# A second level of Strassen in product 4 of both tiles, one more residual by accumulating DMA, and weight loads planned around the accumulations

## The chip, the cores and the metric

The kernel runs on one core of a Trainium2 chip. The metric is the device time of one launch in microseconds (us): the median of several runs. A profile is taken of one execution; its span goes from the first to the last instruction on the core.

The core has a matrix engine (TensorE, PE in the profile; PEld is its loading of weights), a vector engine (VectorE, DVE), a scalar engine (ScalarE, ACT), GpSimd (POOL) and a synchronising engine (SyncE, SP) that here only issues DMAs. Each runs its own list of instructions in order and waits on semaphores for the others. Matrix results go to PSUM, in banks of 128 x 512 floats.

## The reference

A deep cross network of six layers over 16384 rows of 1024 values, with `x0` the input:

```python
x = x0                                   # [16384, 1024] bf16
for l in range(6):
    proj = einsum('bd,de->be', x, ws[l]) + bs[l]     # ws[l]: [1024, 1024]
    x = x0 * proj + x
```

So each layer is one product with a 1024 x 1024 matrix, a bias, a product with `x0` and a residual.

## The kernel before

**Tiling.** The rows are split into 16 pairs of 512-row tiles, 1024 rows a pair. All data is kept transposed (features on partitions). A pair's `x` is a 2 x 2 of blocks: feature half by row tile. Two pairs make a group, and the group's two pairs are called lanes 0 and 1 (the change's words call them tiles). The kernel runs 96 *units*, one layer of one pair, in the order group, layer, lane: layer 0 of lane 0, layer 0 of lane 1, layer 1 of lane 0 and so on. A group is 12 units. The three buffers of `x` (`xst`) and of `x0` (`x0T`) rotate over the pairs.

**One unit.** The 2 x 2 block product is done with seven products instead of eight (the Winograd form of Strassen's algorithm). Their names are P1 to P7. DVE makes the differences T1 to T4 of input blocks; TensorE multiplies them with weights or with sums of weights, which group 0 makes once and saves to device memory (`Lc`). P1, P6, P7 accumulate on each other in four PSUM banks `pA`; each is 16 matmuls of 512 columns (four for each of the output blocks m: P1.0 to P1.3). Products 5, 2 and 3 go one *level* deeper: each is again seven products of half size, 28 matmuls of 256 columns in all, on the banks `pX` (5 and 3 on pX0 and pX1, 2 on pX2 and pX3). The pieces are named 5p1 to 5p7 and so on. Their inputs are made by DVE (5t13, 5t2, 5t4; 23t2 and 23t4 for products 2 and 3 together). ACT evicts PSUM: `biased` (line 335, instruction at 337) adds the bias and writes E1, E6, E7, E4; `copy` (line 326) writes the pieces' results (e_p5, e_c11, e_u0, e_u1, e_c21) and copies bank to bank (f1, f2). DVE then adds the correction `cc`. Product 4 is a 512-column product (P4.0 to P4.3, evicted by E4) or, where `K4` (line 152) lists the lane for a layer, a two-level one (4p1 to 4p7, with 4t13, 4t2, 4t4, 4cc and the add Wa in place of the accumulation on `pA`), on pX2 and pX3. Before, `K4` lists both lanes in layer 0, lane 1 alone in layers 1 to 4, and none in layer 5; group 0 keeps one level.

**End of a unit.** DVE adds products into four result blocks Q, U, V, W (Q1, Ua, Ub, Va, Wa; lines 547 to 555), multiplies each by `x0` (Qm, Um, Vm, Wm) and adds the residual: by DVE (Qx and so on, line 566) or, for the blocks in `DMA_RES` (line 153), by an accumulating DMA that POOL issues (line 563). W is block 21 (second feature half, first row tile). Before, Q, U and V go by DMA in layers 1 to 4, and W by DVE. In layer 0 the products go straight to the buffer, and in layer 5 DVE adds all four. The result is the input of the same lane's next layer, two units later.

**Buffers.** Seven evict buffers hold 5c, 3c (products 5 and 3), U, V, W, Q and P1s (product 1). From unit to unit the names change places by `NEXT` (line 176).

**Order.** Everything is first recorded as an `Op` with an engine, a duration, what it reads and writes. The order on TensorE is written out by hand: `PE_TWO` for units with one-level product 4, `PE_FOUR` for two-level ones, others for the first units and the last. `schedule` (line 51) lays all operations out by these durations, taking on each engine the ready one that is due first; the program is emitted in that order, so every engine has a fixed order. Weights go through a ring of 12 slots of 512 KB (`RING`): 11 loads for each layer of a group (10 in layer 5), in the order of `ring_seq` (line 225). `pump` (line 239) is called after every emitted operation and issues the next load on SP as soon as its slot's last use has been emitted. SP also has the transposing loads of `x0` (`ld`), the output's transposes (`tro`) and stores (`sto`).

Of the kernel before, what the change touches and what calls it, by code (L numbers as in the profile page):

```python
# [20 lines left out]
PE_ONE = """  # L21
# [1 line left out]
P3.0 P4.3 P4.1 P4.0 P4.2  # L23
""".split()
PE_TWO = """
5p5 P1.1 5p1 P1.0 P1.3 5p2 2p5 5p6 2p1 P1.2 5p3 2p2 5p7 2p6 P6.0 5p4 2p3 3p5 2p7 3p1 P6.1 2p4 3p2 3p6 P6.2 P6.3 3p3
3p7 P7.0 P7.1 P7.2 3p4 P7.3 P4.1 P4.0 P4.3 P4.2
""".split()
PE_FOUR = """
5p5 P1.0 5p1 2p5 2p1 P1.1 5p2 5p6 2p2 P1.2 2p6 P1.3 5p3 5p7 2p3 2p7 P6.0 3p5 5p4 2p4 P6.1 P6.3 3p1 4p5 P6.2 4p1 3p2  # L30
P7.0 4p2 3p6 4p6 P7.1 3p3 4p3 4p7 P7.2 3p7 4p4 P7.3 3p4
""".split()
PE_LAST = """
P1.0 P1.1 P1.2 P1.3 P2.0 P2.1 P2.2 P2.3 P5.0 P5.1 P5.2 P5.3 P6.0 P6.1 P6.2 P6.3 P3.0 P3.1 P3.2 P3.3 P7.0 P7.1 P7.2 P7.3
# [2 lines left out]
ARRIVE = {"rows0": 4.9, "w0.1": 6.4, "rows1": 8.9, "rows2": 11.3, "w0.2": 11.9, "h0": 14.3, "h1": 15.5, "q": 17.5, "next": 21.0, "raw1": 40.0}  # L37


ACCUM = 9.0  # L40


class Op:
# [81 lines left out]
    return order, start, late  # L125


@with_exitstack
def kernel(
    ctx: ExitStack,  # L130
# [18 lines left out]
    KQ, HQ, NQ = KH // 2, H // 2, NB // 2  # L149
    RING = 12  # L150
    NDUMMY = 8
    K4 = {0: (0, 1), 1: (1,), 2: (1,), 3: (1,), 4: (1,)}
    DMA_RES = {1: "QUV", 2: "QUV", 3: "QUV", 4: "QUV"}

    const = ctx.enter_context(tc.tile_pool(name="const", bufs=1))
    dram = ctx.enter_context(tc.tile_pool(name="dram", bufs=1, space=bass.MemoryType.DRAM))
# [16 lines left out]
    ip["4"] = ip["2"]  # L173
    P1s, P5s, Q, U, V, W, C3 = (work.tile([P, KH, KH, P], BF16, name=f"ev{i}") for i in range(7))
    EV = {"5c": P5s, "3c": C3, "U": U, "V": V, "W": W, "Q": Q, "P1s": P1s}
    NEXT = {"5c": "3c", "3c": "5c", "U": "W", "V": "U", "W": "V", "Q": "Q", "P1s": "P1s"}
    home = {r: r for r in EV}
    TURNED, rows = ((0, 0), (1, 0), (0, 1)), (P1s, U, V)
    zeros = tin["4"][:, 0]
# [41 lines left out]
    for gl in range(NGROUP * L):  # L221
        if gl < L:
            ring_seq += [(gl, w, "load") for w in RAW] + [(gl, w, "make") for w in MADE]
        else:
            ring_seq += [(gl, w, "load") for w in "1 5 5i 2 2i 6 3 3i 7 4 4i".split()[:11 if gl % L in K4 else 10]]
    slot = {(gl, w): f"slot{i % RING}" for i, (gl, w, _) in enumerate(ring_seq)}
    wt, uses_left, live = {}, {}, []
    pos = {"next": 0}
# [7 lines left out]
        live.append(key)  # L236
        return wt[key]

    def pump():
        while pos["next"] < len(ring_seq):  # L240
            gl, w, kind = ring_seq[pos["next"]]
            if kind == "make":
                return
            t = ring_tile((gl, w))
            if t is None:
                return
            nc.sync.dma_start(t[:], w_src(gl % L, w))
            pos["next"] += 1

    def ring_make(gl, w):  # L250
# [27 lines left out]
    for u, (pr, l) in enumerate(units):  # L278
# [12 lines left out]
        kmajor = l == 0  # L291
        inn = "" if one else "5234" if lane in K4.get(l, ()) and grp > 0 else "523"
        ISW = [ISN[w] for w in ISLOT] + [f"is.{w}.{i}" for w in ISLOT for i in "5637"] if pr == 2 else []
        line = {w: i for i, w in enumerate(PE_FIRST if first else PE_LAST if last else PE_ONE if one else PE_FOUR if lane in K4.get(l, ()) and pr > 1 else PE_TWO)}

        def pe(name, occ, fn, rd, wr, weights=(), u=u, gl=gl, line=line, at=0.0):
            op(f"{name}@{u}", "PE", occ, occ + 0.19, fn, rd, wr, [(gl, w) for w in weights], key=(u, line[name]), at=at)
# [15 lines left out]
        def group(name, w, bank, bname, rhs, rname, m, start, gl=gl, kmajor=kmajor):  # L313
            def fn():
                for k in range(KH):
                    r = rhs[:, k, :] if kmajor else rhs[:, :, k, :]
                    o = bank[:] if kmajor else bank[:].rearrange("p (j r) -> p j r", r=P)
                    nc.tensor.matmul(o, lhsT=wt[(gl, w)][:, k, m * P:(m + 1) * P], rhs=r,  # L318
                                     start=(start and k == 0), stop=(k == KH - 1), skip_group_check=True)
            if first and name in ("P5.0", "P5.1"):  # L320
                rname = rname + ["w0.5a"]
            else:
                rname = rname + wname(w)
            pe(name, 0.863, fn, rname, [bname], [w], at={"1": ARRIVE["w0.1"], "2": ARRIVE["w0.2"]}.get(w, 0.0) if first else 0.0)
# [151 lines left out]
        if not one:  # L476
            for X, a, b in (("5", 0, 1), ("2", 2, 3), ("3", 0, 1), ("4", 2, 3))[:len(inn)]:
                Bm, src = SRC[X]
                C, pn = CB[X], Pn[X]
                if kmajor:  # L480
                    q = lambda dh, n, k, Bm=Bm: Bm[:, dh * KQ + k, n * NQ:(n + 1) * NQ]
                    tk = lambda i, k, X=X: tin[X].rearrange("p i (k b) -> p i k b", k=KQ)[:, i, k]
                else:
                    q = lambda dh, n, k, Bm=Bm: Bm[:, n * KQ:(n + 1) * KQ, dh * KQ + k, :]
                    tk = lambda i, k, X=X: tin[X].rearrange("p i (j k r) -> p i j k r", j=KQ, k=KQ)[:, i, :, k, :]
                c = lambda dh, n, C=C: C[:, n * KQ:(n + 1) * KQ, dh * KQ:(dh + 1) * KQ, :].rearrange("p j m r -> p m j r")
                cn = lambda dh, n, pn=pn: [pn(2 * dh) + f".{n}", pn(2 * dh + 1) + f".{n}"]
                call = [pn(m) for m in range(KH)]

                def inner(i, bank, start, X=X, gl=gl, q=q, tk=tk, src=src, kmajor=kmajor):  # L490
                    quad = {1: (0, 0), 2: (1, 0), 3: (1, 1)}
                    rhs = (lambda k: q(*quad[i], k)) if i in quad else (lambda k: tk({4: 3, 5: 0, 6: 2, 7: 1}[i], k))
                    rn = {1: src, 2: src, 3: src, 4: X + "t4", 5: X + "t13", 6: X + "t2", 7: X + "t13"}[i]
                    w = X if i in (1, 2, 4) else X + "i"

                    def fn():
                        if i in (1, 2, 4):
                            k0, e0 = {1: (0, 0), 2: (KQ, 0), 4: (KQ, HQ)}[i]
                            wv = wt[(gl, w)][:, k0:k0 + KQ, e0:e0 + HQ]
                        else:  # L500
                            wi = weight(gl, w) if gl < L else weight(gl, w)[:]
                            wv = wi.rearrange("p q (k e) -> p q k e", k=KQ)[:, {5: 0, 6: 1, 3: 2, 7: 3}[i]]
                        for m in range(KQ):
                            for k in range(KQ):
                                o = pX[bank][:, m * NQ:(m + 1) * NQ]
                                nc.tensor.matmul(o if kmajor else o.rearrange("p (j r) -> p j r", r=P), lhsT=wv[:, k, m * P:(m + 1) * P],  # L506
                                                 rhs=rhs(k), start=(start and m == 0 and k == 0), stop=(k == KQ - 1), skip_group_check=True)
# [39 lines left out]
        if not last:  # L547
            if not one:
                ttop("Q1", Q[:], Q[:], P1s[:], ADD, allm("Q") + allm("P1s"), allm("Q"))
            ttop("Ua", U[:], U[:], P5s[:], ADD, allm("U") + allm("5c"), allm("U"))  # L550
            if not one:
                ttop("Ub", U[:], U[:], C3[:], ADD, allm("U") + allm("3c"), allm("U"))
            if "4" in inn:
                ttop("Wa", W[:], W[:], V[:], ADD, allm("W") + allm("V"), allm("W"))
            ttop("Va", V[:], V[:], P5s[:], ADD, allm("V") + allm("5c"), allm("V"))
            for nm, C, q in (("Q", Q, (0, 0)), ("U", U, (0, 1)), ("V", V, (1, 1)), ("W", W, (1, 0))):
                if l == 0:
# [148 lines left out]
        load_half("4", h)  # L706
    nc.sync.dma_start_transpose(out=blk(x0Ts[0], 1, 1), in_=x0[NB:2 * NB, H:2 * H])

    held = [i for i in order if ops[i].name.startswith("ld") and ops[i].name.endswith(".1@1")]
    for i in held:  # L710
        ops[i].fn()
    for i in order:
        if i not in held:
            ops[i].fn()
        for k in ops[i].weights:
            if k in uses_left:
                uses_left[k] -= 1
        pump()


# [28 lines left out]
```

## Time and profile before

| | |
|---|---|
| median of 3 runs | 2222.31 us (2222.19 to 2222.82) |
| span of the profiled execution | 2220.2 us |
| PE busy | 2209.2 us, 14565 matmuls |
| PEld busy | 1421.3 us |
| DVE busy | 2133.0 us, 2502 instructions |
| ACT busy | 2035.8 us, 3627 instructions |
| POOL busy | 204.6 us |
| DMA | 478.66 MB, mean 216 GB/s |

The profile gives no launch time of its own for the profiled execution, only its span; 2220.2 us is 2.1 us below the median of the runs. In its lists of instructions an entry reads: line of the kernel, engine, operation, output <- inputs by the names of the tiles, shape, count. The list of waits reads: who waited, for whom, the total in us, how often, the longest. In the list by stretches each engine has its busy time and, in brackets, its instructions. A DMA's landing time counts from the start of the instruction that issues it.

### The profile page before, as it was taken

Reading aid. Unit: us, or ns where it says so; the run is one execution under the profiler, and the core shown is the slowest. Engines: PE = TensorE matmul, PEld = TensorE weight load, DVE = VectorE, ACT = ScalarE, POOL = GpSimd, SP = SyncE. Lnnn points to the kernel's source line nnn. Section 1 sums busy time; section 2 is a strip of 40 time slices with the busy share of each in tenths; the row PEclk is TensorE's granted clock in tenths of the full one; section 3 lists DMA queues with packets and bytes.
Section 4 is the critical chain, followed back from the end, with each engine's and each line's share of the span. In section 5 each row is a group of like instructions: output and inputs, shape, how many; then the busy total and the mean of one; then the engine's idle time right before and its main releaser. Section 6 shows DMA issues by size and latency. Waiting matters only on the chain.

```text
span 2220.2 us, 39424 instructions
## 1 busy us (share of the span) xinstructions
PE 2209.2 (100%) x14565; PEld 1421.3 (64%) x14565; DVE 2133.0 (96%) x2502; ACT 2035.8 (92%) x3627; POOL 204.6 (9%) x263
## 2 busy tenths in 40 slices
PE   9999999999999999999999999999999999999998
PEld 5555566666666666666666666666666666666664
DVE  8999999999999999999999999999999999999997
ACT  7888899999999999999999999999999999999997
POOL 1221100110001100011000110011100111001110
PEclk9999999999999999999999999999999999999999
DMA  9676879767996689966898679986789777897777
GB/s 275 206 204 188 214 202 257 198 174 206 257 258 181 171 226 252 255 176 176 234 250 243 171 189 239 252 223 177 207 232 251 217 179 224 221 259 190 202 224 163
DMA packets 454306, 478.66 MB, mean 216 GB/s; under 512 B 269024, under 2 KB 381152, under 8 KB 454112
## 3 DMA queue, kind: packets, MB, share of 16 engines
q1 hardware_dynamic: 418352, 349.49, 53.3%
q0 software_dynamic: 35168, 126.38, 28.0%
q8 instruction: 114, 1.87, 0.3%
q14 instruction: 80, 0.66, 0.1%
q10 hardware_dynamic: 592, 0.27, 0.0%
HBM read 252.72 MB, written 58.20 MB: 140 GB/s over the span
## 4 chain that ended last, share of the span: by engine, by line
PE 98%; DMA 1%; SPq 0%; DVE 0%; issue 0%; POOLq 0%; ACT 0%; DVEq 0%; ACTq 0%
PE pA L318 53%; PE pX L506 43%; PE pX L318 3%; DMA x0T<-in_x_dram 0%; DMA xst<-x0T 0%; SPq L690 0%; DVE ev L204 0%; SPq L697 0%; DVE x0T L204 0%; DVE T L204 0%; SPq L703 0%; POOLq L744 0%; ACT ev L337 0%; SPq L700 0%; DVEq L204 0%
## 5 line engine op out<-in xcount | busy, mean ns | idle before, releaser
L337 ACT ACTIVATE ev<-pA,b_all 128x512 bf16<-128x512 f32 x1311 | 898.6, 692 | 117.5 <-PE pA L318 78.2
L506 PEld LDWEIGHTS <-wp 128*128 128x128 bf16 x8364 | 818.4, 98 | 270.6 <-issue 1.0
L318 PE MATMUL pA<-T,wp 128*128 128x512 bf16 x3936 | 939.6, 379 | 0.0
L318 PEld LDWEIGHTS <-wp 128*128 128x128 bf16 x5808 | 568.0, 98 | 507.9 <-issue 2.2
L327 ACT CAST ev<-pX 128x512 bf16<-128x512 f32 x1264 | 690.1, 597 | 22.0 <-PE pX L506 14.9
L506 PE MATMUL pX<-ti,wp 128*128 128x256 bf16 x4728 | 655.8, 273 | 0.0
L204 DVE TENSOR_TENSOR ev<-ev,ev 128x2048 bf16<-128x2048 bf16 (+1 forms) x414 | 497.5, 1218 | 44.1 <-ACT ev L327 36.9
L204 DVE TENSOR_TENSOR ev<-ev,x0T 128x2048 bf16<-128x2048 bf16 (+1 forms) x324 | 386.4, 1210 | 1.7 <-ACT ev L337 0.3
L327 ACT COPY pX<-pX 128x512 f32<-128x512 f32 x618 | 359.7, 595 | 3.3
L318 PE MATMUL pA<-xst,wp 128*128 128x512 bf16 x1280 | 318.9, 379 | 0.0
L563 POOL DMA_DIRECT2D xst<-ev x192 | 165.8, 865 | 1292.0 <-ACT ev L337 506.9
L506 PE MATMUL pX<-xst,wp 128*128 128x256 bf16 x1736 | 260.4, 273 | 0.0
L506 PE MATMUL pX<-T,wp 128*128 128x256 bf16 x1548 | 232.2, 273 | 0.0
L204 DVE TENSOR_TENSOR ev<-ev,ip 128x1024 bf16<-128x1024 bf16 x309 | 207.7, 690 | 0.2 <-ACT ev L327 0.2
L204 DVE TENSOR_TENSOR T<-xst,T 128x2048 bf16<-128x2048 bf16 x160 | 195.7, 1223 | 2.4 <-PE pX L506 1.4
L204 DVE TENSOR_TENSOR T<-xst 128x2048 bf16<-128x2048 bf16 x160 | 195.6, 1223 | 1.7 <-PE pA L318 1.4
L327 ACT CAST ip<-pX 128x512 bf16<-128x512 f32 x309 | 182.3, 590 | 0.4 <-PE pX L506 0.4
L204 DVE TENSOR_TENSOR xst<-ev,xst 128x2048 bf16<-128x2048 bf16 x124 | 151.8, 1225 | 0.2
L204 DVE TENSOR_TENSOR ti<-T,ti 128x512 bf16<-128x512 bf16 x262 | 111.2, 424 | 0.2
L204 DVE TENSOR_TENSOR ti<-xst 128x1024 bf16<-128x1024 bf16 x148 | 102.3, 691 | 8.4 <-PE pX L506 8.0
L204 DVE TENSOR_TENSOR ti<-xst,ti 128x1024 bf16<-128x1024 bf16 x148 | 101.9, 689 | 0.1
L204 DVE TENSOR_TENSOR ti<-T 128x1024 bf16<-128x1024 bf16 x131 | 90.4, 690 | 0.1
(57 smaller groups left out, 679.2 us busy)
## 6 DMA issues: line engine op xcount, KB each, us to landing
wp<-Lc SPq DMA_DIRECT2D x329, 512.0 KB, 6.1
xst<-ev POOLq DMA_DIRECT2D x192, 512.0 KB, 5.2
wp<-in_ws_dram SPq DMA_DIRECT2D x148, 512.0 KB, 6.6
out_dram<-x0T SPq DMA_DIRECT2D x60, 512.0 KB, 4.3
Lc<-wp POOLq DMA_DIRECT2D x24, 512.0 KB, 5.1
Lc<-xst POOLq DMA_DIRECT2D x23, 512.0 KB, 5.4
ev<-in_x_dram SPq DMA_DIRECT2D x3, 512.0 KB, 6.1
wp<-in_ws_dram SPq DMA_DIRECT2D x4, 256.0 KB, 7.4
```

The source lines that it names most:

```text
L204: nc.vector.tensor_tensor(out=o, in0=a, in1=b, op=op)
L318: nc.tensor.matmul(o, lhsT=wt[(gl, w)][:, k, m * P:(m + 1) * P], rhs=r, start=(start and k == 0), stop=(k == KH - 1), skip_group_check=True)
L327: act(name, lambda: nc.scalar.copy(out=dst, in_=src), rd, wr)
L337: act(name, lambda: nc.scalar.activation(out=dst, in_=src, func=IDENT, bias=b_all[:, c:c + 1], scale=1.0), rd, wr, True)
L506: nc.tensor.matmul(o if kmajor else o.rearrange("p (j r) -> p j r", r=P), lhsT=wv[:, k, m * P:(m + 1) * P], rhs=rhs(k), start=(start and m ...
L563: nc.gpsimd.dma_start(xblk(xst, *q), C[:], accum_op=ADD)
```

## The change

1. `K4` lists both lanes in layers 0 to 4, so lane 0's product 4 has two levels in layers 1 to 4 too (groups 1 to 7).
2. `DMA_RES` holds W as well: block 21's residual is added by DMA in layers 1 to 4.
3. `plan_loads` gives each weight load from group 1 on a time before which it is not issued: after planned accumulations, but no later than `LEAD` and 1.5 `LOAD` ahead of its first planned use or of the next load's latest time. `pump` gets the time of the operation just emitted and holds loads back by it; a held load also waits for the newest matmul emitted.
4. The ring's order (`LOAD_ORDER`), `PE_TWO`, `PE_FOUR`, the planner's duration for an accumulation (`ACCUM`, 9.0 to 8.5), the rotation `NEXT` and the place of Ua among the recorded operations change. In the new rotation V keeps its buffer, U takes 5c's, 5c takes 3c's, 3c takes W's and W takes U's.

```diff
 PE_TWO = """
-5p5 P1.1 5p1 P1.0 P1.3 5p2 2p5 5p6 2p1 P1.2 5p3 2p2 5p7 2p6 P6.0 5p4 2p3 3p5 2p7 3p1 P6.1 2p4 3p2 3p6 P6.2 P6.3 3p3
-3p7 P7.0 P7.1 P7.2 3p4 P7.3 P4.1 P4.0 P4.3 P4.2
+2p5 5p5 P1.1 5p1 P1.0 P1.3 5p2 5p6 2p1 P1.2 5p3 2p2 5p7 2p6 P6.0 5p4 2p3 3p5 2p7 3p1 P6.1 2p4 P6.3 3p2 3p6 P6.2 P7.1
+3p7 3p3 P7.3 P7.0 3p4 P7.2 P4.0 P4.3 P4.2 P4.1
 PE_FOUR = """
-5p5 P1.0 5p1 2p5 2p1 P1.1 5p2 5p6 2p2 P1.2 2p6 P1.3 5p3 5p7 2p3 2p7 P6.0 3p5 5p4 2p4 P6.1 P6.3 3p1 4p5 P6.2 4p1 3p2
-P7.0 4p2 3p6 4p6 P7.1 3p3 4p3 4p7 P7.2 3p7 4p4 P7.3 3p4
+5p1 P1.0 5p5 P1.2 2p5 2p1 5p6 5p2 P1.1 2p6 2p2 P6.0 5p3 P1.3 5p7 2p3 3p5 2p7 P6.2 5p4 2p4 P6.1 P6.3 3p1 4p5 4p1 P7.0
+3p2 4p2 3p6 4p6 P7.1 3p3 4p3 3p7 4p7 P7.3 3p4 4p4 P7.2
-ACCUM = 9.0
+ACCUM = 8.5
+LOAD, BURST, LEAD = 1.45, 2.9, 5.0
+LOAD_ORDER = "1 5i 2i 5 2 6 3i 4i 3 4 7".split()
+def plan_loads(loads, bursts):
+    latest, nxt = [0.0] * len(loads), 1e9
+    for n in range(len(loads) - 1, -1, -1):
+        nxt = min(loads[n][1] - LEAD, nxt) - 1.5 * LOAD
+        latest[n] = nxt
+    busy, t = [], 0.0
+    for b in sorted(bursts):
+        t = max(t, b + 1.0)
+        busy.append((t, t + BURST))
+        t += BURST
+    issue, t = [], 0.0
+    for n, (free, _) in enumerate(loads):
+        s = max(free, t)
+        limit = max(s, latest[n])
+        for a, b in busy:
+            if b > s and a < s + 0.7 * LOAD:
+                s = b
+        t = min(s, limit)
+        issue.append(t)
+        t += LOAD
+    return issue
-    K4 = {0: (0, 1), 1: (1,), 2: (1,), 3: (1,), 4: (1,)}
-    DMA_RES = {1: "QUV", 2: "QUV", 3: "QUV", 4: "QUV"}
+    K4 = {l: (0, 1) for l in range(L - 1)}
+    DMA_RES = {l: "QUVW" for l in range(1, L - 1)}
-    NEXT = {"5c": "3c", "3c": "5c", "U": "W", "V": "U", "W": "V", "Q": "Q", "P1s": "P1s"}
+    NEXT = {"5c": "3c", "3c": "W", "U": "5c", "V": "V", "W": "U", "Q": "Q", "P1s": "P1s"}
-            ring_seq += [(gl, w, "load") for w in "1 5 5i 2 2i 6 3 3i 7 4 4i".split()[:11 if gl % L in K4 else 10]]
+            ring_seq += [(gl, w, "load") for w in LOAD_ORDER if w != "4i" or gl % L in K4]
-    def pump():
+    def pump(time=0.0):
...
-            if kind == "make":
+            if kind == "make" or held.get((gl, w), 0.0) > time:
                 return
...
-            nc.sync.dma_start(t[:], w_src(gl % L, w))
+            ld = nc.sync.dma_start(t[:], w_src(gl % L, w))
+            if (gl, w) in held:
+                tc.add_manual_dep(ld.ins, newest["pe"].ins.name, mybir.DependencyInfo(mybir.DependencyClass.Sync, mybir.DependencyReason.DATA))
-            ttop("Ua", U[:], U[:], P5s[:], ADD, allm("U") + allm("5c"), allm("U"))
             if not one:
                 ttop("Ub", U[:], U[:], C3[:], ADD, allm("U") + allm("3c"), allm("U"))
             if "4" in inn:
                 ttop("Wa", W[:], W[:], V[:], ADD, allm("W") + allm("V"), allm("W"))
+            ttop("Ua", U[:], U[:], P5s[:], ADD, allm("U") + allm("5c"), allm("U"))
     order, start, _ = schedule(ops)
+    first_use, free_at = {}, {}
+    for i in order:
+        for k in ops[i].weights:
+            first_use.setdefault(k, start[i])
+            free_at[k] = max(free_at.get(k, 0.0), start[i] + ops[i].occ)
+    late_keys = [(n, (gl, w)) for n, (gl, w, _) in enumerate(ring_seq) if gl >= L]
+    plan = plan_loads([(free_at[ring_seq[n - RING][:2]], first_use[k]) for n, k in late_keys],
+                      [start[i] for i, o in enumerate(ops) if o.name[1:3] == "x@" and o.eng == "POOL"])
+    for (_, k), t in zip(late_keys, plan):
+        held[k] = t
...
-        pump()
+        pump(start[i])
```

The new order on the engines follows from the planner. In the units of layers 2 to 4, DVE's order after a unit's end is 4cc, 3cc, Wa, Ub, Wm, Ua, 23t4, Um, Va, 4t13, Vm, T3, 4t2, then 5cc, 2cc, 4t4, Q1, 2t13, Qm, T1, 5t13, 5t2, 5t4, 3t13, T2, 23t2, T4, where cc, a, b, m and Q1 belong to the unit that ends and the t and T to the units that follow. ACT's order at a unit's end is 3e_c11, 4e_c11, 3f2, 4f2, 3e_u0, 4e_u0, 3e_u1, 4e_u1, E7.0, E7.1, 3e_c21, 4e_c21, E7.2, E7.3, and E6.0 comes between 2e_u0 and 2e_u1.

More of the change, by code (lines that the diff above doesn't have):

```diff
@@ L237, in ring_tile @@
         return wt[key]
-    def pump():
+    held, newest = {}, {}
+    def pump(time=0.0):
         while pos["next"] < len(ring_seq):
             gl, w, kind = ring_seq[pos["next"]]
-            if kind == "make":
+            if kind == "make" or held.get((gl, w), 0.0) > time:
                 return
@@ L293 @@
         ISW = [ISN[w] for w in ISLOT] + [f"is.{w}.{i}" for w in ISLOT for i in "5637"] if pr == 2 else []
-        line = {w: i for i, w in enumerate(PE_FIRST if first else PE_LAST if last else PE_ONE if one else PE_FOUR if lane in K4.get(l, ()) and pr > 1 else PE_TWO)}
+        line = {w: i for i, w in enumerate(PE_FIRST if first else PE_LAST if last else PE_ONE if one else PE_FOUR if lane in K4.get(l, ()) and grp > 0 else PE_TWO)}
         def pe(name, occ, fn, rd, wr, weights=(), u=u, gl=gl, line=line, at=0.0):
@@ L317, in fn @@
                     o = bank[:] if kmajor else bank[:].rearrange("p (j r) -> p j r", r=P)
-                    nc.tensor.matmul(o, lhsT=wt[(gl, w)][:, k, m * P:(m + 1) * P], rhs=r,
-                                     start=(start and k == 0), stop=(k == KH - 1), skip_group_check=True)
+                    newest["pe"] = nc.tensor.matmul(o, lhsT=wt[(gl, w)][:, k, m * P:(m + 1) * P], rhs=r,
+                                                    start=(start and k == 0), stop=(k == KH - 1), skip_group_check=True)
             if first and name in ("P5.0", "P5.1"):
@@ L505, in fn @@
                                 o = pX[bank][:, m * NQ:(m + 1) * NQ]
-                                nc.tensor.matmul(o if kmajor else o.rearrange("p (j r) -> p j r", r=P), lhsT=wv[:, k, m * P:(m + 1) * P],
-                                                 rhs=rhs(k), start=(start and m == 0 and k == 0), stop=(k == KQ - 1), skip_group_check=True)
+                                newest["pe"] = nc.tensor.matmul(
+                                    o if kmajor else o.rearrange("p (j r) -> p j r", r=P), lhsT=wv[:, k, m * P:(m + 1) * P],
+                                    rhs=rhs(k), start=(start and m == 0 and k == 0), stop=(k == KQ - 1), skip_group_check=True)
                     if gl < L and w.endswith("i"):
@@ L707 @@
     nc.sync.dma_start_transpose(out=blk(x0Ts[0], 1, 1), in_=x0[NB:2 * NB, H:2 * H])
-    held = [i for i in order if ops[i].name.startswith("ld") and ops[i].name.endswith(".1@1")]
-    for i in held:
+    early = [i for i in order if ops[i].name.startswith("ld") and ops[i].name.endswith(".1@1")]
+    for i in early:
         ops[i].fn()
     for i in order:
-        if i not in held:
+        if i not in early:
             ops[i].fn()
```

## The prediction

> **What bounds the kernel now.** I read the page's first part, then who made TensorE wait, then busy time by stretch, and last the order of time around one unit's start. One unit is one layer for one pair of tiles; a group is twelve units.
>
> ```profile
> span 2220.2 us, 39424 instructions
> ...
> PE 2209.2 (100%) x14565; PEld 1421.3 (64%) x14565; DVE 2133.0 (96%) x2502; ACT 2035.8 (92%) x3627; POOL 204.6 (9%) x263
> ...
> PEclk9999999999999999999999999999999999999999
> ```
> ```profile
> PE pX L681 <- DVE ti L678: 1.2, 1, 1.2
> PE pX L318 <- ACT pX L327: 0.8, 2, 0.5
> ```
> TensorE (PE) is busy all through at full clock. Its longest waits, in total, are 1.2 and 0.8 us, at the start. So time is TensorE work, and work taken from it is time, as long as no other engine comes late.
>
> ```profile
> core 0: us, PE busy (x) PEld busy (x) DVE busy (x) ACT busy (x) POOL busy (x), PEclk, DMA share, GB/s
> 837.00:1110.60 273.60, 273.60 (x1849) 180.81 (x1848) 267.00 (x311) 256.93 (x463) 21.78 (x26) 1.00 0.83 219
> 1160.05:1183.03 22.98, 22.98 (x150) 14.48 (x148) 22.98 (x28) 21.30 (x38) 0.91 (x1) 1.00 1.03 279
> 1183.03:1205.62 22.59, 22.59 (x162) 15.65 (x160) 22.36 (x27) 21.68 (x41) 2.58 (x3) 1.00 0.80 219
> ```
> The first row is a whole group, then a unit with product 4 as one level (22.98 us) and a unit with two levels (22.59 us). VectorE (DVE) is second: 267.0 of 273.6 us, 6.6 us idle in a group.
>
> ```profile
> 1205.97 0.58 ACT L327 CAST ev<-pX 128x512 bf16<-128x512 f32 x1
> ...
> 1206.92 0.60 PE L506 MATMUL pX<-T,wp 128*128 128x256 bf16 x4
> ...
> 1207.44 3.49 DVE L204 TENSOR_TENSOR ev<-ev,ev 128x2048 bf16<-128x2048 bf16 x3
> ...
> 1212.48 1.55 ACT L327 CAST ev<-pX 128x512 bf16<-128x512 f32 x3
> ...
> 1214.30 0.60 PE L506 MATMUL pX<-ti,wp 128*128 128x256 bf16 x4
> ...
> 1214.94 1.08 ACT L327 CAST ev<-pX 128x512 bf16<-128x512 f32 x2 [0.42 <-PE pX L506]
> ...
> 1216.05 0.60 PE L506 MATMUL pX<-xst,wp 128*128 128x256 bf16 x4
> ...
> 1217.12 1.29 DVE L204 TENSOR_TENSOR ev<-ev,ip 128x1024 bf16<-128x1024 bf16 x2
> ...
> 1217.39 1.28 ACT L337 ACTIVATE ev<-pA,b_all 128x512 bf16<-128x512 f32 x2
> ```
> Durations overlap when instructions follow each other, so I take the pitch. DVE: (3.49 - 1.22)/2 = 1.135 us for 128x2048, 1.29 - 0.69 = 0.60 for 128x1024, and by the same step 0.60 - 0.535/2 = 0.33 for 128x512. ScalarE (ACT): (1.55 - 0.60)/2 = 0.475 for a cast, 1.28 - 0.69 = 0.59 for a biased eviction. TensorE: between 1214.30 and 1216.05 lie four groups of four 256-column matmuls, 0.437 us a group ("a p"); the one-level unit has 21 of them and 16 groups of four 512-column matmuls ("a P"): (22.98 - 21 x 0.437)/16 = 0.863. A cast starts 0.04 us after the recorded end of its matmuls (1214.94 against 1214.90).
>
> ```profile
> DVE ev L204 <- ACT ev L327: 37.1, 30, 1.9
> ```
> ```profile
> DMA to landing us min/median/max: 4.5/5.2/9.7
> ```
> ```profile
> DMA to landing us min/median/max: 3.1/6.4/10.2
> ```
> The first line: most of DVE's idle time is waiting for evictions. The other two are the accumulating DMAs (line 563, median 5.2 us from issue to landing) and the weight loads (line 247, 6.4 us).
>
> **TensorE.** In layers 1 to 4 of seven groups the first tile's unit changes: 4 x 7 = 28 units. Sixteen 512-column matmuls (P4.0 to P4.3) become 28 of 256 columns. The two unit rows differ by just this: 22.98 - 22.59 = 0.39 us, with all weight loads in it. 28 x 0.39 = -10.9 us. TensorE waited for nothing there, so the whole of it lies on the path.
>
> [...]
>
> **VectorE work.** A changed unit adds one subtraction of 1024 columns, two of 512, one correction add of 1024 (4t13, 4t2, 4t4, 4cc) and one add of 2048 (Wa): 0.60 + 2 x 0.33 + 0.60 + 1.135 = 3.0 us, 12.0 in a group. Block 21's residual (Wx) leaves DVE in all eight units of layers 1 to 4: -8 x 1.135 = -9.1. Net +2.9: 269.9 us of work in a group of 273.6 - 4 x 0.39 = 272.0. Idle falls from 6.6 to 2.1 us. Cost zero while that cover lasts: a DVE that runs later no longer waits for evictions. If the cover is gone, each us is a us.
>
> **Do VectorE's results still come in time?** I add pitches along the new order, with TensorE's offsets from its own. A unit's tail needs 4cc, 3cc and the last E7; TensorE's last P, then E7.2 and E7.3 on ACT (0.2 + 2 x 0.59 + some queue), put Wa about 1.6 us into the next unit. Wa, Ub, Wm, Ua, 23t4, Um, Va, 4t13, Vm, T3 follow: 8 x 1.135 + 2 x 0.60 = 10.3, T3 ends at 11.9. P7.0 reads it after 8 P and 18 p: 14.8. 2.9 us spare, the least of all of DVE's outputs; 4t13 and 23t4 have over 4. In the layer 5 and layer 0 units, where DVE falls behind most, the same sums leave over 4.
>
> **ScalarE.** Four biased evictions become seven plain ones: 7 x 0.475 - 4 x 0.59 = +0.97 us a unit, 256.9 + 3.9 = 260.8 of 272.0. Cover is ample, but two hand-offs are new. The rotation makes the new U the old 5c buffer, so E6.0 waits for Va of the unit before: 9.1 us against E6.0's place at about 10.0. And TensorE now opens a unit with 5p1, which needs bank pX0, that is 3e_c21; on ACT that stands behind E7.0 and E7.1, put late since V's buffer no longer rotates. From 3p3's end TensorE has 5 p and 2 P left (3.91 us). ACT has 0.16 (0.60 - 0.437) + 0.04 until 3p3's result can be read, 3e_u0, 4e_u0, 3e_u1, 4e_u1 (4 x 0.475), E7.0 and E7.1 (2 x 0.59), 3e_c21 (0.58, and 0.05 to TensorE, estimated from the 0.04): 3.91. Before, that cast ended at 1206.55 and 5p1 ran at 1206.92: 0.37 us spare. Now none. Bounds: 0 (waiting gains nothing) and one more eviction (0.59) at each of 6 such starts in 7 groups, 42 x 0.59 = 25 us. I take 0.02 each, the error of these pitches: +0.8 us, since the sum itself comes out even.
>
> **Accumulating DMA.** 64 more (192 to 256), 0.86 us each on POOL, which is 91% idle. On its queue stand U's and V's behind W's. W's product ends 5.1 us into the next unit, U's 8.0, V's 10.8. Landing after 5.2 us: 10, 13, 16; the first overwrites of their buffers are 3e_c11 (16.3), 4e_c11 (16.8) and E7.0 (20.8), and DVE reads V's block at 18.9. Even 9.7 us is late only for U by 1 and for 3t13 by 1.6. Bounds 0 and 1.6 x 56 = 90 us; I take 0, the median.
>
> **Weight loads.** Their number stays. A load is now kept back past planned accumulations, to no nearer than LEAD + 1.5 LOAD = 7.2 us before planned use, and waits on SP for the newest matmul; behind it on SP stand later loads, the transposing loads and the output transposes and stores; TensorE waits if a weight is late. Median landing 6.4: cost 0. Longest 10.2: 3.0 us at 28 layer starts, 84 us. I take 0, nearer the median, and held loads queue behind fewer others. Group 0 gets the new PE_TWO order (2p5 first, 4.3 us earlier): its inputs stood ready much longer there, and in the first such unit about 3 us remain: 0. The moved adds Ua, the other rotation and the new load order issue nothing more: 0, by the sums above.
>
> **Sum.** Median 2222.3 - 10.9 + 0.8 = 2212.2. The profiled span, 2220.2, stands 2.1 us under the median (what lies around the span), and should become 2210.1.
>
> **Rivals.**
> (a) Slower, VectorE becomes the bound. Idle time stays 6.6 us in a group since evictions now end late in both tiles (for it: 30 such waits, up to 1.9 us; against: DVE would be later then, and not wait). 269.9 + 6.6 = 276.5 against 273.6, seven groups: +20, 2242 us. It costs from 2.1 us of idle time on, and makes the kernel slower by 0.2% from 4.3 (269.9 + 4.3 - 273.6 = 0.6 a group).
> (b) No change: the 5p1 hand-off misses by half an eviction: 42 x 0.3 = 12.6 us, 2224. For it: no spare. Against: the sum is even.
> (c) Slower: held loads land late. Half way between median and longest is 8.3, 1.1 us at 28 starts, 31 us, 2243. For it: DMA share is 0.80 there already and one accumulation more comes on top; against: fewer loads at a time.
> (d) Slower, weight loads stop hiding: the 12 more that a changed unit has, 98 ns each, would add 1.18 us: 28 x (1.18 - 0.39) = +22, 2244 us. The two-level unit row holds them already and is shorter, so 1 in 100.
>
> **How the numbers follow.** Forecast 0.64, (a) 0.13, (b) 0.13, (c) 0.09, (d) 0.01. The bound of what a measurement can tell is 0.2%, 4.4 us. Faster: 0.64 and a part of (b), 0.67; same: 0.10; slower: 0.23. The range goes from the bare gain less some head effects, 2210, past (b) to 2232, which leaves out most of (a) and (c). The forecast's own range is 2210 to 2217.
>
> **What would show it.** Right: units of layers 1 to 4 all 22.6 us, group period 272, DVE idle near 2 us a group, TensorE's waits under 3 us in all, no wait for a weight load. (a) shows as TensorE waiting for T or ti; (b) as pX waiting for ACT; (c) as weight loads of TensorE waiting for DMA. The forecast is wrong if any of these passes 7 us.

## The result and the profile after

The changed kernel takes 2243.5 us (median of four runs, 2242.6 to 2246.9) against 2222.4: a ratio of 1.0098, 95% interval 1.0086 to 1.0110. It is 1% slower. The forecast was 2212.2, so 31.3 us are to be explained: the 10.1 that were to be gained and the 21.2 that were lost. The profiled execution took 2246.9 us with a span of 2245.1; it is 3.4 us above the median.

The page of the profile after, its first part, the queues and the chain that ended last:

```profile
span 2245.1 us, 40162 instructions
...
PE 2211.8 (99%) x14901; PEld 1453.2 (65%) x14901; DVE 2150.9 (96%) x2578; ACT 2035.0 (91%) x3711; POOL 259.9 (12%) x327
...
q1 hardware_dynamic: 418352, 349.49, 54.2%
q0 software_dynamic: 44384, 159.94, 34.4%
...
PE 82%; DMA 7%; DVE 6%; ACT 2%; issue 2%; SPq 0%; POOLq 0%; ACTq 0%; DVEq 0%
```

TensorE (PE) now has 33 us of its span idle, where it had 11. The queue that POOL's accumulating DMAs use (q0) takes 34.4% of the 16 DMA engines' span; it was 28.0%. The chain runs 7% of the span through transfers.

Who made TensorE and its weight loading (PEld) wait, in the list of waits (total, times, longest):

```profile
PE pX L535 <- DMA wp<-in_ws_dram: 5.3, 7, 1.5
PE pA L347 <- DMA wp<-Lc: 4.7, 3, 3.2
PE pX L535 <- ACT pX L356: 4.4, 11, 0.9
PE pA L347 <- DVE ti L229: 2.5, 1, 2.5
```
```profile
PEld L535 <- DMA wp<-in_ws_dram: 8.6, 11, 1.8
PEld L347 <- DMA wp<-Lc: 8.3, 4, 3.5
```

Before, no wait of TensorE was longer than 1.2 us, and that one stood at the start. Now weights come late (`wp`), and ScalarE (ACT) frees banks late. The row with `DVE ti` is a late weight too: this wait, at 354.8 us, ended when a load issued at 352.70 landed after 4.6 us, and PEld's row for the same moment names `wp<-Lc`. With one more row of 0.8 us, TensorE waited 5.3 + 4.7 + 2.5 + 0.8 = 13.3 us for weights. VectorE (DVE) and ACT wait for accumulating DMAs, which had made them wait 0.5 us in all. The first fence is the view of line 593, which issues these DMAs, the second that of line 274, which issues the weight loads (lines 563 and 247 before):

```profile
who waited for it (us, times):
  DVE T L229: 7.1, 5
  ACT ev L356: 4.0, 5
  DVE ti L229: 0.7, 1
...
DMA to landing us min/median/max: 4.5/7.2/11.1
```
```profile
DMA to landing us min/median/max: 3.2/6.0/15.0
```

The accumulating DMA's median went from 5.2 to 7.2 us and its longest from 9.7 to 11.1. Before, 6 of 192 took more than 8.5 us, the time that the planner now gives an accumulation; after, it is 41 of 256. The loads' median fell from 6.4 to 6.0 us, but their longest rose from 10.2 to 15.0. A part of the chain shows how one late transfer spreads (start, duration, what):

```profile
1218.95 10.86 DMA xst<-ev
...
1230.39 0.60 ACT pX L356
1231.04 0.61 PE pX L535 x4
...
1253.36 9.41 DMA wp<-in_ws_dram
```

U's accumulation, issued 0.9 us after W's, took 10.86 us, where the planner counts with 8.5. The cast 4e_c11 on ACT overwrites U's buffer and had to wait for it (1.3 us, to 1229.91); so ACT freed a bank late, and TensorE waited 0.9 us. Later in this chain a load of weight 2, issued one us before Q's accumulation, took 9.41 us and came late too. What was issued from 1217 to 1230 us, in the first 13 us of this (count, size, median us from issue to landing):

```profile
xst<-ev POOLq DMA_DIRECT2D x3, 512.0 KB, 9.5
wp<-Lc SPq DMA_DIRECT2D x1, 512.0 KB, 6.1
wp<-in_ws_dram SPq DMA_DIRECT2D x1, 512.0 KB, 15.0
```

The same stretch of the same unit before, 1211 to 1224 us:

```profile
xst<-ev POOLq DMA_DIRECT2D x3, 512.0 KB, 4.6
```

There three accumulations met no new load and took 4.6 us.

### The profile page after: what moved, and what is told of

It is laid out like the page before. It is cut to its first block, busy times and chain, and to the rows that moved or that the text cites. A ratio compares the mean times of both kernels' runs of the same rounds, so it can differ in the third digit from the quotient of the medians.

```text
span 2245.1 us, 40162 instructions
## 1 busy us (share of the span) xinstructions
PE 2211.8 (99%) x14901; PEld 1453.2 (65%) x14901; DVE 2150.9 (96%) x2578; ACT 2035.0 (91%) x3711; POOL 259.9 (12%) x327
## 3 DMA queue, kind: packets, MB, share of 16 engines
q0 software_dynamic: 44384, 159.94, 34.4%
## 4 chain that ended last, share of the span: by engine, by line
PE 82%; DMA 7%; DVE 6%; ACT 2%; issue 2%; SPq 0%; POOLq 0%; ACTq 0%; DVEq 0%
PE pA L347 41%; PE pX L535 38%; DVE ev L229 4%; PE pX L347 3%; DMA wp<-in_ws_dram 3%; DMA xst<-ev 2%; DMA wp<-Lc 2%; DVE ti L229 1%; DVE T L229 1%; ACT ev L366 1%; ACT ev L356 1%; ACT pX L356 0%; DMA x0T<-in_x_dram 0%; SPq L730 0%; DMA xst<-x0T 0%
## 5 line engine op out<-in xcount | busy, mean ns | idle before, releaser
L535 PEld LDWEIGHTS <-wp 128*128 128x128 bf16 x9148 | 893.8, 98 | 325.3 <-issue 18.1
L366 ACT ACTIVATE ev<-pA,b_all 128x512 bf16<-128x512 f32 x1199 | 817.0, 709 | 76.0 <-PE pA L347 62.9
L347 PE MATMUL pA<-T,wp 128*128 128x512 bf16 x3488 | 856.4, 379 | 7.2 <-DMA wp<-Lc 4.7
L356 ACT CAST ev<-pX 128x512 bf16<-128x512 f32 x1376 | 760.3, 603 | 76.2 <-PE pX L535 60.3
L347 PEld LDWEIGHTS <-wp 128*128 128x128 bf16 x5360 | 523.8, 98 | 442.1 <-DMA wp<-Lc 8.3
L535 PE MATMUL pX<-ti,wp 128*128 128x256 bf16 x5176 | 714.8, 273 | 0.8 <-ACT pX L356 0.2
L229 DVE TENSOR_TENSOR ev<-ev,ev 128x2048 bf16<-128x2048 bf16 (+1 forms) x442 | 527.5, 1213 | 10.6 <-ACT ev L356 6.1
L356 ACT COPY pX<-pX 128x512 f32<-128x512 f32 x674 | 387.2, 586 | 12.6 <-PE pX L535 2.2
L593 POOL DMA_DIRECT2D xst<-ev x256 | 221.0, 863 | 1259.5 <-ACT ev L356 552.7
L535 PE MATMUL pX<-T,wp 128*128 128x256 bf16 x1884 | 283.0, 273 | 3.5 <-ACT pX L356 1.9
L229 DVE TENSOR_TENSOR xst<-ev,x0T 128x2048 bf16<-128x2048 bf16 x64 | 76.8, 1217 | 0.0
```

Of the source, the lines that this page charges most:

```text
L229: nc.vector.tensor_tensor(out=o, in0=a, in1=b, op=op)
L347: newest["pe"] = nc.tensor.matmul(o, lhsT=wt[(gl, w)][:, k, m * P:(m + 1) * P], rhs=r, start=(start and k == 0), stop=(k == KH - 1), skip_ ...
L356: act(name, lambda: nc.scalar.copy(out=dst, in_=src), rd, wr)
L366: act(name, lambda: nc.scalar.activation(out=dst, in_=src, func=IDENT, bias=b_all[:, c:c + 1], scale=1.0), rd, wr, True)
L535: newest["pe"] = nc.tensor.matmul(o if kmajor else o.rearrange("p (j r) -> p j r", r=P), lhsT=wv[:, k, m * P:(m + 1) * P], rhs=rhs(k), sta ...
L593: nc.gpsimd.dma_start(xblk(xst, *q), C[:], accum_op=ADD)
```

## The experiments

Times of before on these chips were 2222.2 to 2222.4; intervals are 95%. "Accumulations" are the DMAs of line 593.

### First round: is the hold the fault?

Holding back is undone (`e1`), weights are led further (`e2`), W's residual is left out (`e3`), and product 4 alone is changed in the kernel before (`e4`).

```diff
e1_no_hold
-        held[k] = t
+        pass
e2_lead9
-LOAD, BURST, LEAD = 1.45, 2.9, 5.0
+LOAD, BURST, LEAD = 1.45, 2.9, 9.0
e3_no_w_residual (in the loop that adds the residuals)
+                if nm == "W" and nm in DMA_RES.get(l, ""):
+                    continue
e4_two_levels_only (against the kernel before)
-    K4 = {0: (0, 1), 1: (1,), 2: (1,), 3: (1,), 4: (1,)}
+    K4 = {l: (0, 1) for l in range(L - 1)}
```

> The changed kernel without the hold: a load is issued as soon as its slot's last use is done, as before the change; all else as changed. Theory H (the hold brings weights too close to their use: spare 0 to 1.2 us for weights 5 and 2, about 17 us of TensorE's waits in the profile are for weights): these waits vanish, 2226 us or less, 7 us of the rest being ScalarE coming late. Theory D (the fourth accumulation overloads the DMA engines, whenever loads are issued): the loads collide with the accumulations instead, accumulations land later than the 7.2 us median of the changed kernel, TensorE waits for ScalarE and VectorE in place of weights, 2240 us or more.

> The changed kernel with LEAD 9.0 in place of 5.0: a load is held to no nearer than 11.2 us before its planned use, in place of 7.2. Theory H: weights 5 and 2 have about 4 us more to spare, no wait for a weight is left, 2226 to 2230 us. Theory D: the same number of transfers in the same time, 2240 us or more.

> The changed kernel without block 21's residual in layers 1 to 4 (it is left out of the computation, on VectorE and by DMA alike), so 192 accumulations as before the change and the hold around them. Theory H: the hold still brings weights late, 10 to 17 us of waits for weights are left, 2225 to 2230 us; the waits for ScalarE behind late accumulations go. Theory D: landings fall back to 5.2 us, no stall is left but the 5p1 hand-off (0.09 us at 42 starts), 2212 to 2216 us.

> The kernel before with the second level of product 4 in both lanes and nothing else: W stays on VectorE, old orders, old rotation, no hold. VectorE gets 12.0 us more in a group and nothing is taken from it: 267.0 + 12.0 = 279 us against the 273.6 of before, so by both theories it becomes the bound: 2222 + 7 x 5.4 = 2260 us, with TensorE waiting for T, ti and, through late eviction buffers, for ScalarE. If it is 2212 instead, VectorE's sums are wrong and the fourth accumulation was not needed.

Measured: without holding 2302.1 us (1.0362, 1.0343 to 1.0381); with LEAD 9 2269.9 (1.0221, 1.0204 to 1.0238); without W's residual 2249.5 (1.0118, 1.0103 to 1.0133); product 4 alone 2311.0 (1.0398, 1.0382 to 1.0413).

The waits for accumulations without holding, and with LEAD 9:

```profile
DVE ti L229 <- DMA xst<-ev: 42.6, 18, 3.6
...
ACT ev L356 <- DMA xst<-ev: 33.1, 22, 4.0
PE pX L535 <- ACT pX L356: 32.9, 34, 3.6
...
DVE T L229 <- DMA xst<-ev: 24.3, 21, 3.3
```
```profile
DVE ti L229 <- DMA xst<-ev: 40.1, 24, 2.8
```

Without holding no weight was late, but accumulations were, and that costs far more: 59 us over the changed kernel. Both times are in theory D's range, but its sign failed: the accumulations' medians are 6.5 and 7.1 us, not over 7.2. It is the slow end that grew: 79 and 67 of 256 took more than 8.5 us, where it was 41 in the changed kernel. So the hold is not the fault; it protects the accumulations, and LEAD is a balance between late weights and late accumulations.

Product 4 alone costs 89 us. Its 12 us of VectorE work a group come to 267.0 + 12.0 = 279.0 by the prediction's pitches (278.0 busy in the group from 863.0 to 1149.5 us), more than the 272.0 that TensorE then needs, so some work had to leave VectorE. But that sum gave 2260 us, and the run is 51 us above it. This group took 286.5 us, with VectorE idle for 8.5 of it, and in the whole run `T` waited 50.8 us for accumulations, of which there are only three a unit. How much of the 89 us is VectorE's load is not shown.

The run without W's residual missed both theories and settled nothing: with these operations left out the planner lays all others out anew, TensorE waited 10.2 us for `ACT ev`, for which it had waited 0.2, and weights were still late.

### Second round: are transfers in each other's way?

In the first three runs the order on TensorE, ScalarE and VectorE is kept, and one kind of transfer is taken away. `f1` loads no weights from layer 5 of group 1 on and uses those of before it; `f2` cuts all accumulations to one partition, `f3` only W's, so most of that residual is missing. `g1` makes the planner reckon with later accumulations, which changes the order.

```diff
f1_no_loads
-    for gl in range(NGROUP * L):
+    for gl in range(2 * L - 1):
...
-        gl, grp, lane = gl_of(u), pr // 2, pr % 2
+        gl, grp, lane = min(gl_of(u), 2 * L - 2), pr // 2, pr % 2
f2_small_accumulations
-                        nc.gpsimd.dma_start(xblk(xst, *q), C[:], accum_op=ADD)
+                        nc.gpsimd.dma_start(xblk(xst, *q)[0:1], C[0:1], accum_op=ADD)
f3_small_w_accumulation
-                    def acc(C=C, q=q, xst=xst):
-                        nc.gpsimd.dma_start(xblk(xst, *q), C[:], accum_op=ADD)
+                    def acc(C=C, q=q, xst=xst, few=slice(0, 1 if nm == "W" else P)):
+                        nc.gpsimd.dma_start(xblk(xst, *q)[few], C[few], accum_op=ADD)
g1_planned_landing_10_5
-ACCUM = 8.5
+ACCUM = 10.5
```

> The changed kernel without weight loads from layer 5 of group 1 on: all later layers multiply with the weights of layer 4 that lie in the ring (the loads and so the right weights are left out). The order on PE, ACT, DVE and POOL stays. Theory C (weight loads and accumulations slow each other on the DMA engines, so that either the accumulations land after the planned 8.5 us or the held weights come after their use): with no loads, accumulations land in 4.5 to 7 us, no wait for weights and none of ScalarE behind accumulations is left after group 1; only the 5p1 hand-off of 0.09 us at some 42 starts and group 1's own waits stay: 2215 to 2219 us. Theory P (the new orders and rotation have too little spare by themselves, and the DMAs only show it): of 31 us only the 17 us of waits for weights go, 2226 us or more.

> The changed kernel with every accumulating DMA cut to one partition of 128 (the rest of the residual in layers 1 to 4 is left out); order, loads and hold as changed. Theory C: weights 5, 2 and 7 land in 4 to 6 us and in time, ScalarE waits for no accumulation, 2214 to 2218 us. Theory P: 2226 us or more.

> The changed kernel with only block 21's accumulating DMA cut to one partition (its residual is left out); Q, U and V accumulate as before, order, loads and hold as changed. Theory C: the fourth accumulation is what fills the DMA engines; most of the 31 us of waits goes, 2215 to 2225 us. Theory P: no change, about 2240 us.

> The changed kernel with ACCUM 10.5 in place of 8.5: the planner puts what needs an accumulation later in the order of ScalarE and VectorE, for the landings of 9 to 11 us that the trace shows. Theory C: ScalarE no longer stands blocked behind late landings; weights as late as before, so 2232 to 2240 us, unless the later evictions cost TensorE more. Theory P: the spare is smaller still, 2250 us or more.

Measured: 2224.6 us without loads (ten runs, 2220.8 to 2228.1), 2223.1 with all accumulations small (ten, 2221.5 to 2225.4), 2227.1 with W's small (ten, 2223.5 to 2231.4), 2264.2 with the later planned landing (1.0187, 1.0171 to 1.0202).

The landings: accumulations without the loads, then loads without the accumulations.

```profile
DMA to landing us min/median/max: 4.5/4.8/9.6
```
```profile
DMA to landing us min/median/max: 3.1/4.5/10.9
```

Each kind alone lands early: accumulations in 4.8 us at the median instead of 7.2, loads in 4.5 instead of 6.0. (The 9.6 us in `f1` was issued at 474 us, while weights still came.) Taking away either kind removes about the same 19 to 20 us (2243.5 - 2224.6 = 18.9; 2243.5 - 2223.1 = 20.4). They are not two costs that add; it is one cost, of the two together. W's accumulations, the ones that the change adds, bring 16.4 of it (2243.5 - 2227.1). Two rows of the list by stretches show it in group 4 (from one layer 0 to the next), first of the changed kernel, then of the one with small accumulations:

```profile
1121.20:1396.83 275.63, 273.57 (x1897) 185.10 (x1896) 270.80 (x323) 256.69 (x475) 28.68 (x34) 1.00 0.90 231
```
```profile
1116.63:1389.17 272.54, 272.54 (x1898) 185.39 (x1897) 270.77 (x324) 256.02 (x475) 25.23 (x34) 1.00 0.62 171
```

The columns are the stretch, its length, busy time of PE, PEld, DVE, ACT and POOL, the granted clock, the DMA engines' share and GB/s. The work of VectorE and ScalarE is the same in both; with a DMA share of 0.90 the group is 3.1 us longer. Before, the share in such a group was 0.83.

Making the planner expect 10.5 us did not help: `T` on VectorE still waits 19.5 us for accumulations (7.1 in the changed kernel), and TensorE waits 9.2 us for `ACT pX` (4.4). This run came out where theory P had it, so the small spare of the order matters as well.

Both theories missed in one thing: with one kind of transfer gone the kernel is not at 2212, but at 2223 to 2225, between the ranges of C and P. Some 11 us lie elsewhere.

### Third round: what is left, and can it be mended?

In `h1` (all accumulations small, as in `f2`) and in the next two runs TensorE begins a two-level unit with P1.0 instead of 5p1. `h2` and `h4` are the whole kernel: `h2` also puts P7.0 behind 3p2, `h4` also lets weights 2 and 7 be issued 1.5 us earlier. `h3` puts the second level and W's DMA into one layer of the kernel before.

```diff
h1_hand_off (on f2) and h4: PE_FOUR
-5p1 P1.0 5p5 P1.2 2p5 2p1 5p6 5p2 P1.1 2p6 2p2 P6.0 5p3 P1.3 5p7 2p3 3p5 2p7 P6.2 5p4 2p4 P6.1 P6.3 3p1 4p5 4p1 P7.0
+P1.0 5p1 5p5 P1.2 2p5 2p1 5p6 5p2 P1.1 2p6 2p2 P6.0 5p3 P1.3 5p7 2p3 3p5 2p7 P6.2 5p4 2p4 P6.1 P6.3 3p1 4p5 4p1 P7.0
h2_p7_later: PE_FOUR
-5p1 P1.0 5p5 P1.2 2p5 2p1 5p6 5p2 P1.1 2p6 2p2 P6.0 5p3 P1.3 5p7 2p3 3p5 2p7 P6.2 5p4 2p4 P6.1 P6.3 3p1 4p5 4p1 P7.0
-3p2 4p2 3p6 4p6 P7.1 3p3 4p3 3p7 4p7 P7.3 3p4 4p4 P7.2
+P1.0 5p1 5p5 P1.2 2p5 2p1 5p6 5p2 P1.1 2p6 2p2 P6.0 5p3 P1.3 5p7 2p3 3p5 2p7 P6.2 5p4 2p4 P6.1 P6.3 3p1 4p5 4p1
+3p2 P7.0 4p2 3p6 4p6 P7.1 3p3 4p3 3p7 4p7 P7.3 3p4 4p4 P7.2
h4_lead_2_7, besides
-    plan = plan_loads([(free_at[ring_seq[n - RING][:2]], first_use[k]) for n, k in late_keys],
+    plan = plan_loads([(free_at[ring_seq[n - RING][:2]], first_use[k] - (1.5 if k[1] in "27" else 0.0)) for n, k in late_keys],
h3_one_layer (against the kernel before)
-    K4 = {0: (0, 1), 1: (1,), 2: (1,), 3: (1,), 4: (1,)}
-    DMA_RES = {1: "QUV", 2: "QUV", 3: "QUV", 4: "QUV"}
+    K4 = {0: (0, 1), 1: (0, 1), 2: (1,), 3: (1,), 4: (1,)}
+    DMA_RES = {1: "QUVW", 2: "QUV", 3: "QUV", 4: "QUV"}
```

> The kernel with accumulations cut to one partition (2223.1 us; it leaves out most of the residual of layers 1 to 4), with one change: in PE_FOUR the piece 5p1 and P1.0 change places, so TensorE has 0.87 us of other work before it needs the bank that 3e_c21 frees. Theory H (the hand-off costs what its trace shows: 3.8 us of TensorE's idle time stand before 5p1, units are 22.67 instead of 22.59): 2223.1 - 3.8 = 2219.3, units 22.59, no gap at 5p1; 2218.5 to 2220.5. Rival S (ScalarE is late there by itself and the same time then stands before the next piece that waits for it): 2222 to 2224, units stay 22.67.

> The changed kernel with 5p1 behind P1.0 and P7.0 one piece later (behind 3p2, 0.44 us). Theory C (the 20 us over the kernels without one kind of transfer are transfers beside each other): only the hand-off goes and a part of the late weights of product 7 (8 us in all, 4 waits): 2243.5 - 3.8 - 2 = 2238; 2235 to 2241. Rival L (two late starts are the cause, and each drags later ones with it): 2222 to 2230.

> The changed kernel with 5p1 behind P1.0 and the planned first use of weights 2 and 7 put 1.5 us earlier, so their loads may be issued 1.5 us sooner. Theory C: the late weights (16.8 us) fall by half, but accumulations meet more loads (from 14 us of waits for ScalarE to about 20): 2243.5 - 3.8 - 8 + 6 = 2238; 2233 to 2243. Rival L (weight loads late is a fault of its own, without a price elsewhere): 2243.5 - 3.8 - 15 = 2225; 2221 to 2229.

> The kernel before with product 4 on two levels in both tiles and W's residual by DMA in layer 1 alone; orders, rotation and loads as before. Theory C with a threshold (14 more accumulations among 192 raise the DMA engines' share by about 1.6 points, and the transfers still land): 7 x 0.39 = 2.7 us of TensorE's work gone, 2222.2 - 2.7 = 2219.5; 2218.5 to 2221. Rival P (each layer brings its share of the loss): (2243.5 - 2222.3) / 4 = 5.3 us, 2227.5; 2225 to 2232.

Measured: 2220.8 us for `h1` (eleven runs, 2217.8 to 2222.4; 0.9993 of before, 0.9984 to 1.0002); 2249.2 for `h2` (1.0118, 1.0104 to 1.0132); 2258.1 for `h4` (1.0156, 1.0142 to 1.0170); 2259.5 for `h3` (1.0170, 1.0156 to 1.0184).

Group 4 of `h1`, in the same columns:

```profile
1118.45:1390.46 272.01, 271.64 (x1891) 185.52 (x1897) 270.34 (x323) 256.50 (x476) 25.23 (x34) 1.00 0.63 171
```

It is 272.01 us, where the forecast had 272.0; so are groups 2, 5 and 6, and group 3 is 272.8. The group was 272.54 with 5p1 first: the hand-off costs 0.53 a group, 3.7 us in seven. (In the medians it is 2.3; the runs of each of the two kernels scatter over 4 us.) The cause is in the order of time, here of the kernel with small accumulations at a unit's start:

```profile
1206.17 1.03 PE L347 MATMUL pA<-T,wp 128*128 128x512 bf16 x4
...
1206.44 1.11 ACT L356 CAST ev<-pX 128x512 bf16<-128x512 f32 x2
...
1207.12 0.60 PE L535 MATMUL pX<-T,wp 128*128 128x256 bf16 x4
```

The first of the two casts is 3e_c21. At 0.60 us it ends at 1207.04, and 5p1 starts 0.08 us behind it. The four matmuls of P7.2 before it began at 1206.17, so they stand 0.95 us ahead of 5p1 instead of the usual 0.863: TensorE loses nearly 0.09 us there (0.53 / 6 = 0.088), at 42 starts. The modelled ends of matmuls hide this; no row of this trace shows it as idle time.

`h2` and `h4` missed on both sides. The mend of the hand-off is lost in the whole kernel. With P7.0 later, weights of the pieces were late more (TensorE's first row in the list of waits):

```profile
PE pX L535 <- DMA wp<-in_ws_dram: 12.9, 15, 2.0
```

With weights 2 and 7 earlier they were hardly late, but accumulations were, and ScalarE behind them:

```profile
PE pX L535 <- ACT pX L356: 12.2, 41, 0.6
...
DVE ti L229 <- DMA xst<-ev: 21.5, 16, 3.0
```

Its order on TensorE, ScalarE and VectorE is that of `h1`; full accumulations and 1.5 us of lead for two loads in eleven are the difference between 2258 and 2221.

`h3` missed too, and says most. It adds 16 accumulations to 192 (one for each of 16 pairs; the expectation had 14), so the mean DMA share in a group hardly changes (0.84 to 0.85; it was 0.83), yet the run is 37 us longer. The place is one unit in each of seven groups (layer 1, lane 1). In the third group, the accumulations on POOL and the first two weight loads on SP, first in `h3`, then in the kernel before, where TensorE's order shows the unit 3.9 us earlier:

```profile
645.26 0.86 POOL L563 DMA_DIRECT2D xst<-ev  x1 [9.86 <-ACT ev L327]
648.42 0.85 POOL L563 DMA_DIRECT2D xst<-ev  x1 [2.30 <-ACT ev L327]
649.93 0.85 POOL L563 DMA_DIRECT2D xst<-ev  x1 [0.65 <-DVE ev L204]
656.58 0.85 POOL L563 DMA_DIRECT2D xst<-ev  x1 [5.80 <-ACT ev L327]
...
646.88 1.66 SPq L247 DMA_DIRECT2D wp<-Lc  x2
```
```profile
639.73 0.87 POOL L563 DMA_DIRECT2D xst<-ev  x1 [7.51 <-ACT pX L327]
641.53 0.85 POOL L563 DMA_DIRECT2D xst<-ev  x1 [0.93 <-DVE ev L204]
651.78 0.86 POOL L563 DMA_DIRECT2D xst<-ev  x1 [9.40 <-ACT pX L327]
...
643.02 1.21 SPq L247 DMA_DIRECT2D wp<-Lc  x2
```

The medians of these accumulations, again `h3` first, then the slow one in the chain of `h3` and the list of waits:

```profile
xst<-ev POOLq DMA_DIRECT2D x4, 512.0 KB, 11.1
```
```profile
xst<-ev POOLq DMA_DIRECT2D x3, 512.0 KB, 8.0
```
```profile
649.93 13.69 DMA xst<-ev
```
```profile
DVE T L204 <- DMA xst<-ev: 28.5, 7, 5.4
```

In both runs six loads are issued in 7.4 us, at the same places of the unit. Before, two accumulations go out 3.3 and 1.5 us ahead of the first load. In `h3` only one goes out ahead of it, and two follow 1.5 and 3.0 us behind it, among the loads; these took 11.4 and 13.69 us, and `T` on VectorE waited for an accumulation in each of the seven groups, up to 5.4 us. The run's mean granted clock is 0.995, where it was 0.999 before; 0.004 of its 2256.9 us of span is an estimate of 9 us among the 37. So what decided here is not the mean share, but that accumulations which are awaited went out among loads. In the order of before and without loads held back, one layer costs more (37 us) than four layers do in the changed kernel (21).

## Why the prediction was wrong, step by step

- **TensorE, -10.9 us: right.** A two-level unit is 22.59 us and a group 272.01 once nothing waits: 273.58 - 272.01 = 1.57 a group, 11.0 in seven. The two unit rows that it was read from, 22.59 against 22.98 us, held.
- **VectorE's work and results, 0: right.** It is busy 270.8 us in the group (269.9 forecast) and keeps up in 272.0. Rival (a) is out. So is (d): weight loading hides as before, a load at 98 ns on the page before and after, and 185.52 us of loading in a group of 272.01 (`h1`; 180.83 in 273.58 before).
- **ScalarE's hand-off, +0.8: mechanism right, size wrong.** "The sum comes out even" gave 0.02 a start; 0.088 was measured, 3.7 us in all. With no spare, whatever the sum is short of falls on TensorE at every start. Some 0.03 of it is the step from the cast to 5p1 (0.08 us, estimated at 0.05); where the rest comes from is not shown. Rival (b) was priced at 0.3. ScalarE's busy time did not rise to 260.8 us in a group as the pitches said: it is 256.7, and was 256.9. Nothing hung on it.
- **Accumulating DMA, 0, and weight loads, 0: the step that failed.** Both were priced by the medians of the kernel before, 5.2 and 6.4 us, as if each transfer kept its duration while 64 were added and loads were pressed into what time was left. Accumulations went to 7.2, the load's longest to 15.0, and the two together cost 19 to 20 us. One place of it the prediction had named itself: U's accumulation ahead of 4e_c11, late by 1 us if it took 9.7; it took 10.86 in the chain above. Rival (c), at 0.09, named the late weights. That its time, 2243, is the measured one is luck: it is 31 us of late weights, and TensorE waited 13.3 us for weights; the rest is late accumulations, the hand-off and the end. Nor did it see that leaving the loads alone would be worse (2302), because then the accumulations are late. The bounds, 90 and 84 us, held it; the choice "nearer the median" did not. The trace of before already had the sign: accumulations took from 4.5 to 9.7 us and loads from 3.1 to 10.2. Taking one kind away (`f1`, `f2`) shows that much of this is the company that a transfer has (medians of 4.8 us alone against 7.2, and 4.5 against 6.0), and the change added company.
- **Output and transposes on SP, 0: wrong by 1.5 to 4.4 us in group 1.** They were named as queued behind held loads; it was the other way round. SP spent 4.2 us on issuing a transpose just before the load of weight 7, which was issued only 2.1 us before TensorE came to it at 354.8, where the hold means to leave 7.2, and took 4.6 us (SP's order of time in the changed kernel):

```profile
347.76 0.53 SPq L274 DMA_DIRECT2D wp<-in_ws_dram  x1
348.39 4.22 SPq L691 DMA_TRANSPOSE x0T<-xst  x1
352.70 0.53 SPq L274 DMA_DIRECT2D wp<-Lc  x1
```

  The unit took 25.3 us here, 27.1 with small accumulations (2.6 of it idle, and a granted clock of 0.94 in the unit) and 24.1 in `h1`, instead of 22.6. That it is the transpose's issue is read from the trace; no run took it away.
- **The end, no step at all: 3.9 us.** TensorE's last record ends at 2213.1 and the span at 2220.2 before, 2234.1 and 2245.1 after: 7.1 and 11.0 us. The last stored block of pair 14 (`out_dram<-x0T`) was issued at 2206.7 before, 6.3 us ahead of TensorE's end, and at 2231.8 after, 2.3 us ahead. The three last stores on SP then took 5.5 us at the median instead of 3.2. That the new order of layer 5 makes that pair's blocks later, and so the end, is only read; no run took it away.

The account closes on the kernel with small accumulations: 2222.3 - 11.0 + 3.7 (hand-off) + 4.4 (weight 7 in group 1, 27.05 against 22.67) + 3.5 (end, 10.6 against 7.1 us) = 2222.9; measured 2223.1. The last two terms are of one profiled execution, and runs differ: for that of `h1` the same sum, with 1.5 us for weight 7, 0.8 us in group 3 and 4.3 us for the end, is 2222.3 - 11.0 + 1.5 + 0.8 + 4.3 = 2217.9, and it took 2218.0, but the median of `h1` is 2220.8; what makes its runs differ by up to 4.6 us is not shown. The other 20.4 us up to 2243.5 are the transfers in each other's way. So even with nearly all of the accumulations' bytes gone and the hand-off mended (`h1`) the median is within what can be told from no change: the gain on TensorE is real, and the small costs eat most of it before the large one comes.

None of the versions that do the whole work beats the kernel before. Whether another order of loads lets four accumulations a unit land in time stays open.

## What to carry to other kernels

Where the DMA engines are as busy as here (0.83 in a group before the change), a transfer's duration in the trace is its duration in that company: accumulations took 7.2 us at the median beside the loads and 4.8 without them. Price added transfers from the slow end of the spread, count how many land later than the plan allows, and look at what is issued in the 10 us around each transfer that an engine waits for, not at the mean share or the median. Moving work from a full engine to an idle queue was not free here, since the queue's transfers and the loads made each other late, which cost 19 to 20 us. And a hand-off whose times sum to zero spare lost a little at every occurrence (0.088 us at 42 starts), so count occurrences.

## What the hardware showed that was not expected

- A 512 KB weight load that takes 3.2 us at its best took 15.0 us among three accumulations, and 17.5 in the kernel without holding. An accumulation of 512 KB takes 4.5 us at its best, up to 11.1 in the changed kernel, and 13.69 in the chain of `h3` above.
- One late weight cost more than its wait. P7.0 in a unit of group 6 waited 3.2 us, and the next 3.4 us had a granted clock of 0.50 (column after POOL):

```profile
1826.40:1829.90 3.50, 0.27 (x3) 0.13 (x3) 3.40 (x4) 0.57 (x1) 0.77 (x1) 1.00 0.82 166
1829.90:1833.30 3.40, 3.40 (x15) 1.97 (x14) 1.56 (x4) 0.78 (x2) 0.09 (x1) 0.50 0.89 157
```

  A shorter wait did it too: with small accumulations (`f2`), behind a wait of 2.6 us at 354.5 us, four matmuls of 512 columns took 1.89 us, where four from 361.38 us on took 1.03; the unit's granted clock was 0.94. In the changed kernel one of 2.5 us at the same place did not: from 357.4 to 360.8 us the clock was 1.00. From 1226 to 1231 us, in the chain shown above, TensorE idled 0.9 us, and the clock stayed at 1.00. What decides it is not shown.
